# Decoding 64-bit weights: low bits taken by ScalarE, and pieces of 512 columns instead of 256 until the folding is done

## The chip, the cores and the metric

One core of one Trainium2 chip runs one launch of the kernel. The metric is device time in microseconds, from the first instruction to the end of the launch. Engines are called as in the profile: PE (TensorE; PEld is its weight load), DVE (VectorE), ACT (ScalarE), POOL (GpSimd), SP (SyncE, which here issues most of the DMAs).

## What is computed

A recurrent attention over 768 steps, for 4 batches of 8 heads with a 40x40 state each, then two dense blocks without a norm or a residual:

```python
for t in range(S):                                   # 768
    y[:, :, t] = einsum('bhd,bhde->bhe', r_t, state)
    Sa = einsum('bhde,bhe->bhd', state, a_t)
    state = state * w_t[:, :, None, :] - einsum('bhd,bhe->bhde', Sa, b_t) + einsum('bhd,bhe->bhde', v_t, k_t)
x = y as (3072 tokens, 320)
h = (x @ w1) * (x @ w2) @ w3                         # w1, w2: 320x1024, w3: 1024x1024
x = h @ w_out                                        # 1024x320
out = maximum(x @ w_in, 0) ** 2 @ w_out2             # 320x2048, 2048x320
```

The weights of the dense blocks come as 64-bit floating-point numbers (a weight is a 32-bit draw times a 64-bit scalar), everything else as 32-bit.

## The kernel before

**Stages.** The 768 steps are cut into 24 chunks of 32 (`NCH`, `C`). A chunk is a chain of small matmuls on PE with evictions between them: `do_x0` (L737), `do_sa` (L747, evicted to `SA` by ACT at L749), `do_sat` (L754, evicted at L756 and L759), `do_l` (L767, evicted to `YI` by DVE at L772), `do_z` (L780) and `do_ys` (L795, evicted by DVE: the new state at L803, the outputs at L807). `do_sa` needs a small triangular inverse, which `solve` computes on DVE for four chunks at a time: pairs of L651 and L654, step by step, and a transpose (L657) that hands the result to the chunks. `solve(0)` runs in the opening, `solve(1)` beside chunks 2 to 4. `prep` (scans on DVE at L551 and L561, products on POOL at L573 and L579) makes ready the inputs of later chunks.

**Filling.** PE's order is the order of the program (`manual_schedule`): between the chunk's matmuls `stage` pulls a given number of nanoseconds of other PE work from a queue (`Fill`). First in it is the folding, `w3 @ w_out` into one 1024x320 matrix (`fold`, `step`, the matmuls of L455): 64 steps in chunks 0 to 3. Behind it come the first dense block, in 12 tiles of 256 tokens (`a_tile`: matmuls of L366 into `ab`, `g` and `gl` on DVE at L398 and L404, `gh` on ACT, then `px` at L424). The second dense block (`ph` at L366, `po` at L992) runs after all chunks. DVE, ACT, POOL and SP are ordered by a scheduler; each then works through its list in order, and an instruction that waits holds up all behind it.

**Decoding.** `fetch` brings a piece of a weight matrix as raw 32-bit words (two for a number) and makes a 32-bit number of each pair: ACT takes the high word as a float and scales its exponent (L324), DVE shifts left by 3 and clears the sign (L326), ors in the top 3 bits of the low word (L328), and ors in the sign (L330). In the opening the three DVE steps are held back until `solve(0)` is done (`hold`, `issue_after`). The raw words lie in a ring (`raw`), except the first pieces of a kind, which are staged in memory that later holds other tiles (`staged`, tile `early`). `wo` comes in 16 pieces of 160 columns, `w3` in 32 of 256 (2 blocks of 128), `w1` and `w2` in 20 of 256, and, after the folding, `w_in` in 20 of 256 and `w_out2` in 16 of 320. The rings hold 6 raw pieces and 8 decoded ones, and 3 for `w1`/`w2` (`WB`); the first 10 pieces of `w3` are asked for before the chunks begin (`W3_FIRST`), the others one after every second folding step. `w1`, `w2` and `w_in` are then split in two parts: ACT copies one (L338, L349), POOL subtracts it from the whole (L339, L350); `w_out2` likewise (L937, L938).

Of the kernel before, what the change touches and what calls it, by code (L numbers as in the profile page):

```python
# [18 lines left out]
DM = 320  # L19
# [30 lines left out]
SPLIT_AT = (14, 22, 22, 31)  # L50
W3_FIRST = 10
FOLD_STAGED = 16
SPLIT_STAGED = 16
# [7 lines left out]
GAPE = (1300, 2400, 1700, 1600, 1600, 1300, 1000, 2400)  # L61
CUT = (7, 18)
LOOK = (1, 0, 2, 1, 5, 2)
WB = (6, 8, 3)
# [178 lines left out]
def body(tc, img, rv, rd, vn, vp, raw, w1, w2, w3t, wo, win, wo2, ident, maskt, out, dbg=None):  # L243
# [4 lines left out]
    with (  # L248
# [12 lines left out]
        with right, tc.manual_schedule(engines={mybir.EngineType.PE}):  # L261
# [8 lines left out]
            def staged(pl, tags):  # L270
# [23 lines left out]
            def fetch(pl, K, N, parts, dst=None, tag="fold"):  # L294

                place = None
                if early:
                    count[tag] += 1
                    if tag == "split" and count[tag] <= SPLIT_STAGED:
                        place = staged(ma, ("gh", "gl"))  # L300
                    elif tag == "fold" and not w12 and count[tag] <= FOLD_STAGED:
                        place = staged(wa, ("w1h", "w1l", "w2h"))
# [31 lines left out]
            def split_w(pl, src, h, l, j, k):  # L334

                t = fetch(pl, 1, 256, [(slice(0, 128), 0, wcols(src, 256 * j, 256)[128 * k:128 * k + 128])], tag="split")
                f = slice(256 * j, 256 * j + 256)
# [3 lines left out]
            def split_r(pl, two):  # L341


                t = fetch(pl, 1, 256, [(slice(64 * i, 64 * i + 64), 0, wcols(src, c, 256)[256:320])
                                       for i, (src, c, _) in enumerate(two)], tag="split")
                for i, (_, c, r) in enumerate(two):
                    p, q = slice(64 * i, 64 * i + 64), slice(64 - 64 * i, 128 - 64 * i)
                    f = slice(c, c + 256)
# [90 lines left out]
            def fold(solved):  # L439
# [5 lines left out]
                def load_w3(i):  # L445
                    f, g = i // 4, i % 4
                    w3[i] = fetch(wf, 2, 128, [(slice(0, 128), slice(0, 2), wcols(w3t, 128 * f, 128)[
                        256 * g:256 * g + 256, :].rearrange("(k p) f -> p k f", p=128))])

                def step(f, k):  # L450
# [3 lines left out]
                    i = 4 * f + k // 2  # L454
                    mm(out=ps, lhsT=w3[i][:, k % 2], rhs=wo_sb[:, k], start=(k == 0), stop=(k == 7))  # L455
# [4 lines left out]
                def split12(j):  # L460
# [17 lines left out]
                for f in range(8):  # L478
                    for k in range(8):
                        items.append((FOLD_NS, lambda f=f, k=k: step(f, k), "w"))  # L480
                        i = 4 * f + k // 2 + W3_FIRST
                        if k % 2 and i < 32:
                            items.append((0, lambda i=i: load_w3(i), "decode"))
                        if k % 2:
                            for j in range(4):
                                if SPLIT_AT[j] == 4 * f + k // 2:
                                    items.append((0, lambda j=j: split12(j), "decode"))
# [644 lines left out]
```

## Time and profile before

| | |
|---|---|
| median of 3 runs | 1086.69 us (1085.41 to 1086.9) |
| the profiled execution | 1085.28 us, its span 1083.4 us |
| PE busy | 920.8 us (85%) |
| DVE busy | 740.9 us (68%) |
| ACT busy | 420.1 us (39%) |
| POOL busy | 239.6 us (22%) |

How to read it: an engine's busy share over the whole span says little here, since the program has four stretches: the opening, chunks 0 to 3 with the folding, the other chunks filled with the first dense block, and the second dense block. The engine that sets the pace is found per stretch, from busy times by window and from the waits of PE.

### The profile page before, as it was taken

How to read it: one execution, taken by the hardware profiler on the slowest of the kernel's cores; microseconds unless marked ns; L12 is line 12 of the kernel's file. 1: busy time of each engine (PE TensorE's matmuls, PEld its weight loads, DVE VectorE, ACT ScalarE, POOL GpSimd, SP SyncE). 2: the span in 40 equal slices, each digit the busy share in tenths (PEclk: the TensorE clock that was granted, in tenths of full speed). 3: DMA queues.
4: the chain of work that ended last, by engine and by line, in shares of the span. 5: the costliest groups of instructions: out<-in, count | busy, mean ns of one | idle time of the engine just before them, and what ended most of it. 6: DMA issues, size and time to landing. Idle time of an engine off the chain costs nothing.

```text
span 1083.4 us, 29473 instructions
## 1 busy us (share of the span) xinstructions
PE 920.8 (85%) x12240; PEld 825.1 (76%) x12240; DVE 740.9 (68%) x1571; ACT 420.1 (39%) x918; POOL 239.6 (22%) x316
## 2 busy tenths in 40 slices
PE   1326768669999998988999999879999999999997
PEld 1315545558888887877898888869998989898896
DVE  6795889947985996699569544798555564434432
ACT  2313444433334434333343343565433333333332
POOL 0260234613344334433310000454000000000000
PEclk9999888879989999988999998999999999999998
DMA  8977767546657756665764453458112221000001
GB/s 204 287 201 226 192 210 194 143 143 181 149 146 178 193 154 145 165 154 141 172 155 100 113 127 73 121 163 180 30 46 64 62 48 19 7 25 1 19 7 27
DMA packets 211804, 134.46 MB, mean 124 GB/s; under 512 B 144318, under 2 KB 186687, under 8 KB 211249
## 3 DMA queue, kind: packets, MB, share of 16 engines
q1 hardware_dynamic: 204304, 110.61, 40.5%
q0 software_dynamic: 7072, 21.57, 7.1%
q8 instruction: 98, 1.61, 0.7%
q10 hardware_dynamic: 288, 0.33, 0.1%
q14 instruction: 42, 0.34, 0.1%
HBM read 99.27 MB, written 33.19 MB: 122 GB/s over the span
## 4 chain that ended last, share of the span: by engine, by line
PE 54%; DVE 22%; DMA 7%; issue 3%; ACT 2%; SPq 1%; POOL 0%; ACTq 0%; DVEq 0%
PE ph L366 17%; PE po L992 16%; PE ab L366 9%; DVE tmp L651 3%; PE px L424 3%; DVE T L654 3%; PE pat L795 3%; DMA X_d<-yst 2%; DVE RX L803 2%; DVE yst L807 2%; DMA xr<-X_d 2%; DVE wst L328 1%; DVE wst L330 1%; PE pat L780 1%; PE pat L767 1%
## 5 line engine op out<-in xcount | busy, mean ns | idle before, releaser
L992 PE MATMUL po<-wul,rh 128*128 128x320 f32 x384 | 118.4, 309 | 0.0
L992 PE MATMUL po<-wuh,rh 128*128 128x320 f32 x384 | 118.1, 308 | 0.0
L992 PE MATMUL po<-wuh,rl 128*128 128x320 f32 x384 | 117.0, 308 | 0.0
L366 PE MATMUL ab<-xh,w1h 128*128 128x256 f32 x192 | 60.5, 315 | 23.1 <-DVE g L398 22.1
L366 PE MATMUL ph<-xh,wih 128*128 128x512 f32 x192 | 76.6, 399 | 3.1 <-issue 3.1
L403 ACT CAST gh<-g 128x256 fp32r<-128x256 f32 x96 | 39.0, 406 | 99.6 <-DVE g L398 99.4
L366 PE MATMUL ph<-xh,wil 128*128 128x512 f32 x192 | 76.2, 397 | 0.0
L366 PE MATMUL ph<-xl,wih 128*128 128x512 f32 x192 | 76.1, 397 | 0.0
L992 PEld LDWEIGHTS po<-wul,rh 128*128 128x128 f32 x384 | 72.1, 188 | 4.2
L992 PEld LDWEIGHTS po<-wuh,rh 128*128 128x128 f32 x384 | 72.0, 188 | 3.8
L992 PEld LDWEIGHTS po<-wuh,rl 128*128 128x128 f32 x384 | 71.8, 188 | 0.0
L651 DVE TENSOR_TENSOR tmp<-PT,T 128x31 f32<-128x31 f32 (+20 forms) x170 | 68.6, 404 | 3.2
L579 POOL TENSOR_TENSOR im<-im,suf 104x256 f32<-104x256 f32 x80 | 66.0, 852 | 9.5 <-DVE wo_sb L328 5.0
L654 DVE TENSOR_TENSOR T<-T,tmp 128x31 f32<-128x31 f32 (+20 forms) x170 | 65.1, 383 | 2.6
L424 PE MATMUL px<-wph,gh 128*128 128x320 f32 x192 | 64.4, 336 | 2.4 <-ACT gh L403 2.4
L404 DVE TENSOR_TENSOR gl<-g,gh 128x256 fp32r<-128x256 f32 x96 | 44.3, 462 | 28.6 <-ACT gh L403 28.4
L795 PE MATMUL pat<-YI,YR 128*40 128x72 f32 (+1 forms) x1536 | 55.9, 234 | 8.3 <-DVE YI L772 4.4
L398 DVE TENSOR_TENSOR g<-a_sb,ab 128x256 f32<-128x256 f32 x96 | 39.8, 414 | 33.1 <-ACT a_sb L397 32.2
L424 PE MATMUL px<-wph,gl 128*128 128x320 f32 x192 | 60.8, 317 | 1.2 <-DVE gl L404 1.2
L795 PEld LDWEIGHTS pat<-YI,YR 128*40 128x40 f32 x1536 | 51.6, 123 | 13.4 <-issue 5.2
L397 ACT COPY a_sb<-ab 128x256 f32<-128x256 f32 x96 | 35.5, 370 | 66.1 <-PE ab L366 65.7
L366 PE MATMUL ph<-xq,wir 128*128 128x512 f32 x192 | 60.6, 397 | 0.0
(539 smaller groups left out, 2497.5 us busy)
## 6 DMA issues: line engine op xcount, KB each, us to landing
raw<-w3t SPq DMA_DIRECT2D x32, 256.0 KB
YR<-KB_d SPq DMA_DIRECT2D x48, 160.0 KB
im<-img POOLq DMA_DIRECT2D x28, 240.0 KB, 4.8
wt<-AW_d SPq DMA_DIRECT2D x24, 214.5 KB
raw<-wo SPq DMA_DIRECT2D x16, 320.0 KB
RX<-vp SPq DMA_DIRECT2D x24, 208.0 KB
vs<-rv SPq DMA_DIRECT2D x24, 208.0 KB
KB_d<-kn POOLq DMA_DIRECT2D x14, 320.0 KB, 5.5
```

Source lines behind the costliest of these rows:

```text
L366: mm(out=ps, lhsT=seq[i][0], rhs=seq[i][1], start=(i == 0), stop=(i == 7))
L397: act.copy(out=a_sb, in_=ps[:, 0])
L398: dve.tensor_tensor(out=g, in0=a_sb, in1=ps[:, 1], op=ALU.mult)
L403: act.copy(out=t["gh"][:, ff], in_=g)
L404: dve.tensor_tensor(out=t["gl"][:, ff], in0=g, in1=t["gh"][:, ff], op=ALU.subtract)
L424: mm(out=ps, lhsT=a_, rhs=b_, start=(k == 0 and i == 0), stop=(k == 7 and i == 2))
L579: eng.tensor_tensor(out=kb[:, g, :, :, j], in0=kb[:, g, :, :, j], in1=sg, op=ALU.mult)
L651: dve.tensor_tensor(out=tv, in0=Pv[:, :, s, s + 1:n].unsqueeze(3).to_broadcast(sh), in1=Tv[:, :, s, 0:s + 1].unsqueeze(2).to_broadcast(sh) ...
L654: return dve.tensor_tensor(out=o, in0=o, in1=tv, op=ALU.subtract).ins
L795: mm(out=ps[64 * y:64 * y + D, b, 72 * z:72 * z + n], lhsT=YR[:, u], rhs=YI[:, u, 0:n], start=True, stop=True, tile_position=(0, 64 * y))
L803: dve.tensor_tensor(out=o, in0=v[r, :, :, C:72], in1=decay.unsqueeze(3).to_broadcast([D, 2, HZ, D]), op=ALU.mult)
L992: mm(out=po[j][g], lhsT=a_, rhs=b_, start=(ff == 0 and i == 0), stop=(ff == 15 and i == 2))
```

## The change

It does two things. The three DVE steps of decoding become two: ACT makes the top 3 bits of the low word by arithmetic, in place on the raw words (convert to float, times 2^-29, plus a bias just above -0.5, converted back to a whole number by rounding), and one DVE instruction shifts the high part and ors these bits in; the clearing of the sign falls away, as the shift drops it. This holds for all weights. And up to the end of the folding the pieces are twice as wide: `wo` 8 of 320, `w3` 16 of 4x128, `w1` and `w2` 10 of 512. The rings are halved in pieces (3 raw, 4 decoded, 2 for `w1`/`w2`), `W3_FIRST` and the points at which `w1` and `w2` are fetched (`SPLIT_AT`) are restated in the new pieces. A staging tile now gives three places for `wo` (640 words each), so that all 8 pieces have a place; before, 12 of the 16 had one at a time.

```diff
-SPLIT_AT = (14, 22, 22, 31)
-W3_FIRST = 10
-FOLD_STAGED = 16
-SPLIT_STAGED = 16
+SPLIT_AT = (8, 13)
+W3_FIRST = 5
+FOLD_STAGED = 8
+SPLIT_STAGED = 8
+LOW = 2.0 ** -21 - 0.5
-WB = (6, 8, 3)
+WB = (3, 4, 2)
...
-                    t = pl.tile([128, 4, 512], U32, name="early", tag=tags[n[0] % len(tags)])
+                    t = pl.tile([128, 2048], U32, name="early", tag=tags[n[0] % len(tags)])
-                    slots.extend(t[:, i] for i in range(4))
+                    slots.extend(t[:, i:i + words] for i in range(0, 2049 - words, words))
...
                 act.activation(out=o, in_=hi.bitcast(F32), func=AF.Copy, scale=2.0 ** -112)
+                act.activation(out=lo, in_=lo, func=AF.Copy, scale=2.0 ** -29, bias=LOW)
                 with tc.issue_after(hold[-1]) if hold else nullcontext():
-                    dve.tensor_scalar(out=ou, in0=ou, scalar1=3, scalar2=0x7FFFFFFF, op0=ALU.logical_shift_left,
-                                      op1=ALU.bitwise_and)
-                    dve.scalar_tensor_tensor(out=ou, in0=lo, scalar=29, in1=ou, op0=ALU.logical_shift_right,
+                    dve.scalar_tensor_tensor(out=ou, in0=ou, scalar=3, in1=lo, op0=ALU.logical_shift_left,
                                              op1=ALU.bitwise_or)
...
             def split_w(pl, src, h, l, j, k):
+                n = 512 if early else 256
-                t = fetch(pl, 1, 256, [(slice(0, 128), 0, wcols(src, 256 * j, 256)[128 * k:128 * k + 128])], tag="split")
+                t = fetch(pl, 1, n, [(slice(0, 128), 0, wcols(src, n * j, n)[128 * k:128 * k + 128])], tag="split")
...
                 def load_w3(i):
-                    f, g = i // 4, i % 4
-                    w3[i] = fetch(wf, 2, 128, [(slice(0, 128), slice(0, 2), wcols(w3t, 128 * f, 128)[
+                    f, g = i // 2, i % 2
+                    w3[i] = fetch(wf, 4, 128, [(slice(0, 128), slice(0, 4), wcols(w3t, 128 * f, 128)[
...
-                for i in range(16):
-                    c = 160 * (i % 2)
-                    fetch(wf, 1, 160, [(slice(0, 128), 0, wcols(wo, c, 160)[128 * (i // 2):128 * (i // 2) + 128])],
+                for i in range(8):
+                    fetch(wf, 1, DM, [(slice(0, 128), 0, wcols(wo)[128 * i:128 * i + 128, :])], dst=wo_sb[:, i:i + 1])
```

The scheduler also sets other orders. (In the changed kernel the lines below `fetch` are shifted by 2 to 4: ACT's two decoding steps stand at L325 and L326, DVE's at L328 and L330.) Three places count. The first is ACT in the opening, around chunk 0's eviction of `do_sa` into `SA`. Before:

```order
L739 ACTIVATE X_101<-pat 128x320
L692 ACTIVATE x_759<-pat 128x128
L696 COPY tt<-pat 16x8x16 x4
L596 COPY Pn<-pat 128x2x4x32
L324 ACTIVATE wo_sb<-early 128x160 x4
L749 COPY SA<-pat 128x8x40
```

and in the changed kernel:

```order
L741 ACTIVATE X_101<-pat 128x320
L694 ACTIVATE x_683<-pat 128x128
L698 COPY tt<-pat 16x8x16 x4
L325 ACTIVATE wst<-raw 128x512
L326 ACTIVATE raw<-raw 128x512 x3
L598 COPY Pn<-pat 128x2x4x32
L326 ACTIVATE raw<-raw 128x512
L751 COPY SA<-pat 128x8x40
```

The last four pieces of `wo`, which had to wait for a staging place, no longer stand ahead of `SA`; five steps on `w3` pieces, for which a place in the raw ring must come free, now do.

The second is DVE at the end of `solve(1)`, the transpose that chunk 4 waits for. Before, from the step with 3x29 on:

```order
L654 TENSOR_TENSOR T<-T,tmp 128x3x29
L326 TENSOR_SCALAR wst<-wst 128x256
L651 TENSOR_TENSOR tmp<-PT,T 128x60
L328 SCALAR_TENSOR_TENSOR wst<-raw,wst 128x256
L654 TENSOR_TENSOR T<-T,tmp 128x2x30
L330 SCALAR_TENSOR_TENSOR wst<-raw,wst 128x256
L651 TENSOR_TENSOR tmp<-PT,T 128x31
L326 TENSOR_SCALAR wst<-wst 128x320
L654 TENSOR_TENSOR T<-T,tmp 128x31
L328 SCALAR_TENSOR_TENSOR wst<-raw,wst 128x320
L657 STREAM_TRANSPOSE tt<-T 128x8x32
```

and in the changed kernel:

```order
L809 TENSOR_TENSOR yst<-pat,wt 40x2x4x32 x2
L330 SCALAR_TENSOR_TENSOR wst<-raw,wst 128x256
L656 TENSOR_TENSOR T<-T,tmp 128x3x29
L402 TENSOR_TENSOR g<-a_sb,ab 128x256
L330 SCALAR_TENSOR_TENSOR wst<-raw,wst 128x320
L653 TENSOR_TENSOR tmp<-PT,T 128x60
L408 TENSOR_TENSOR gl<-g,gh 128x256
L656 TENSOR_TENSOR T<-T,tmp 128x2x30
L653 TENSOR_TENSOR tmp<-PT,T 128x31
L656 TENSOR_TENSOR T<-T,tmp 128x31
L402 TENSOR_TENSOR g<-a_sb,ab 128x256
L659 STREAM_TRANSPOSE tt<-T 128x8x32
```

Chunk 3's last outputs (`yst`) now stand directly ahead of the solve's last steps, not seven of its steps earlier, and the decoding steps of `w_in` and `w_out2` among them are fewer.

The third is SP's list at the same place, the first pieces of `w_in` and `w_out2` (called `wo` there). Before, behind chunk 3's output to memory:

```order
L810 DMA X_d<-yst 40x4x128
L318 DMA raw<-win 128x512 x2
L377 DMA xf<-X_d 128x2x256
L379 DMA xr<-X_d 64x256 x2
L318 DMA raw<-win 64x512 x2
L318 DMA raw<-wo 128x640 x2
```

and in the changed kernel, ahead of chunk 3's `YR` and `YI` loads and of its output:

```order
L319 DMA raw<-win 128x512 x2
L319 DMA raw<-win 64x512 x2
L602 DMA Q_d<-qt 128x256
L319 DMA raw<-wo 128x640 x2
L616 DMA KB_d<-kn 128x640
L319 DMA raw<-win 128x512
L716 DMA YR<-KB_d 64x2x320
```

These loads moved forward by a dozen DMAs.

## Rows read from the trace of the kernel before

**Rows 1.** Busy time by window: PE, PEld, DVE, ACT, POOL, clock, DMA share, GB/s.
```profile
84.00:145.00 61.00, 42.35 (x866) 31.84 (x866) 42.29 (x99) 20.94 (x56) 13.64 (x16) 0.87 0.74 207
145.00:227.00 82.00, 53.86 (x818) 40.16 (x818) 78.69 (x200) 35.52 (x90) 36.59 (x42) 0.79 0.68 189
227.00:690.00 463.00, 427.03 (x7706) 395.95 (x7707) 332.70 (x754) 180.37 (x422) 126.81 (x193) 0.95 0.57 142
690.00:726.00 36.00, 26.29 (x185) 25.04 (x184) 35.87 (x79) 21.75 (x56) 19.78 (x21) 0.95 0.56 163
726.00:760.00 34.00, 34.00 (x173) 29.99 (x174) 30.15 (x57) 20.22 (x44) 16.07 (x15) 0.95 0.80 169
```

**Rows 2.** Waits of PE, 0 to 260 us: total, times, longest.
```profile
PE pat L747 <- DVE tt L657: 14.4, 1, 14.4
PE pat L754 <- ACT SA L749: 14.2, 2, 8.2
...
PE pat L737 <- DVE RX L803: 4.4, 2, 3.2
```

**Rows 3.** DVE by form, 145 to 227 us: the decoding steps (busy, mean ns).
```profile
L330 DVE SCALAR_TENSOR_TENSOR wst<-raw,wst 128x256 uint32<-128x256 uint32 x22 | 10.8, 495 | 0.0
L328 DVE SCALAR_TENSOR_TENSOR wst<-raw,wst 128x256 uint32<-128x256 uint32 x21 | 10.6, 510 | 0.0
L326 DVE TENSOR_SCALAR wst<-wst 128x256 uint32<-128x256 uint32 x31 | 9.6, 316 | 2.0 <-ACT wst L324 1.9
L328 DVE SCALAR_TENSOR_TENSOR wst<-early,wst 128x256 uint32<-128x256 uint32 x10 | 5.0, 510 | 0.0
L330 DVE SCALAR_TENSOR_TENSOR wst<-early,wst 128x256 uint32<-128x256 uint32 x10 | 4.0, 409 | 0.0
```

**Rows 4.** Timeline of DVE: start, duration, instruction.
```profile
70.47 1.72 DVE L330 SCALAR_TENSOR_TENSOR wo_sb<-early,wo_sb 128x160 uint32<-128x160 uint32 x7
72.12 0.74 DVE L330 SCALAR_TENSOR_TENSOR wst<-raw,wst 128x256 uint32<-128x256 uint32 x2
...
186.29 0.41 DVE L328 SCALAR_TENSOR_TENSOR wst<-early,wst 128x256 uint32<-128x256 uint32 x1
186.63 0.28 DVE L326 TENSOR_SCALAR wst<-wst 128x256 uint32<-128x256 uint32 x1
186.83 0.41 DVE L654 TENSOR_TENSOR T<-T,tmp 128x255 f32<-128x255 f32 x1
```

**Rows 5.** Timeline of DVE at the end of `solve(1)`: waits in brackets.
```profile
223.90 0.29 DVE L326 TENSOR_SCALAR wst<-wst 128x256 uint32<-128x256 uint32 x1 [1.92 <-ACT wst L324]
```

**Rows 6.** POOL by form, 145 to 227 us: the subtractions that split `w2`.
```profile
L339 POOL TENSOR_TENSOR w2l<-wst,w2h 128x256 fp32r<-128x256 f32 x8 | 7.9, 996 | 12.9 <-PE pat L688 9.6 <-ACT w2h L338 3.2
```

**Rows 7.** Timelines of ACT and DVE in chunk 0.
```profile
77.73 0.35 ACT L324 ACTIVATE wo_sb<-early 128x160 f32<-128x160 f32 x1 [5.89 <-DMA early<-wo]
...
80.33 0.41 ACT L749 COPY SA<-pat 128x320 f32<-128x320 f32 x1
...
89.60 1.39 DVE L772 TENSOR_TENSOR YI<-pat,msk 64x512 f32<-64x512 f32 x2
```

**Rows 8.** Waits of PE, 690 to 727 us.
```profile
PE ab L366 <- DVE g L398: 5.2, 2, 3.6
PE ph L366 <- issue: 3.1, 1, 3.1
```

**Rows 9.** DVE by form, 690 to 726 us: the step that goes.
```profile
L326 DVE TENSOR_SCALAR wst<-wst 128x256 uint32<-128x256 uint32 x11 | 5.5, 502 | 0.0
...
L326 DVE TENSOR_SCALAR wst<-wst 128x320 uint32<-128x320 uint32 x8 | 3.7, 460 | 0.0
```

**Rows 10.** ACT by form, whole span: the decoding step on ACT (mean ns).
```profile
L324 ACT ACTIVATE wst<-raw 128x256 f32<-128x256 f32 x56 | 24.4, 439 | 33.9 <-DMA raw<-win 11.2 <-PE pw L455 10.0 <-DMA raw<-w3t 8.0
...
L324 ACT ACTIVATE wo_sb<-early 128x160 f32<-128x160 f32 x16 | 5.6, 347 | 21.6 <-DMA early<-wo 20.9
```

**Rows 11.** Timeline of DVE at the change to the second block.
```profile
725.32 0.50 DVE L429 STREAM_TRANSPOSE x<-px 128x320 f32<-128x320 f32 x1
```

More of the change, by code (lines that the diff above doesn't have):

```diff
@@ L299, in fetch @@
                     if tag == "split" and count[tag] <= SPLIT_STAGED:
-                        place = staged(ma, ("gh", "gl"))
+                        place = staged(ma, ("gh", "gl"), 1024)
                     elif tag == "fold" and not w12 and count[tag] <= FOLD_STAGED:
-                        place = staged(wa, ("w1h", "w1l", "w2h"))
+                        place = staged(wa, ("w1h", "w1l", "w2h"), 640)
                 tag = "split" if early and tag == "split" else "wst"
@@ L334, in split_w @@
             def split_w(pl, src, h, l, j, k):
-                t = fetch(pl, 1, 256, [(slice(0, 128), 0, wcols(src, 256 * j, 256)[128 * k:128 * k + 128])], tag="split")
-                f = slice(256 * j, 256 * j + 256)
+                n = 512 if early else 256
+                t = fetch(pl, 1, n, [(slice(0, 128), 0, wcols(src, n * j, n)[128 * k:128 * k + 128])], tag="split")
+                f = slice(n * j, n * j + n)
                 act.copy(out=h[:, k, f], in_=t[:, 0])
@@ L341, in split_r @@
             def split_r(pl, two):
-                t = fetch(pl, 1, 256, [(slice(64 * i, 64 * i + 64), 0, wcols(src, c, 256)[256:320])
+                n = 512 if early else 256
+                t = fetch(pl, 1, n, [(slice(64 * i, 64 * i + 64), 0, wcols(src, c, n)[256:320])
                                        for i, (src, c, _) in enumerate(two)], tag="split")
@@ L347, in split_r @@
                     p, q = slice(64 * i, 64 * i + 64), slice(64 - 64 * i, 128 - 64 * i)
-                    f = slice(c, c + 256)
+                    f = slice(c, c + n)
                     act.copy(out=r[p, f], in_=t[p, 0])
@@ L453, in step @@
                     ps = w3["ps"]
-                    i = 4 * f + k // 2
-                    mm(out=ps, lhsT=w3[i][:, k % 2], rhs=wo_sb[:, k], start=(k == 0), stop=(k == 7))
+                    i = 2 * f + k // 4
+                    mm(out=ps, lhsT=w3[i][:, k % 4], rhs=wo_sb[:, k], start=(k == 0), stop=(k == 7))
                     if k == 7:
@@ L466, in split12 @@
                             split_w(wf, src, *t[0:2], j, k)
-                    split_r(wf, [(src, 256 * j, t[2]) for src, t in zip((w1, w2), w12)])
+                    split_r(wf, [(src, 512 * j, t[2]) for src, t in zip((w1, w2), w12)])
                 hold.append(solved)
-                for i in range(16):
-                    c = 160 * (i % 2)
-                    fetch(wf, 1, 160, [(slice(0, 128), 0, wcols(wo, c, 160)[128 * (i // 2):128 * (i // 2) + 128])],
-                          dst=wo_sb[:, i // 2:i // 2 + 1, c:c + 160])
+                for i in range(8):
+                    fetch(wf, 1, DM, [(slice(0, 128), 0, wcols(wo)[128 * i:128 * i + 128, :])], dst=wo_sb[:, i:i + 1])
                 for i in range(W3_FIRST):
@@ L480, in fold @@
                         items.append((FOLD_NS, lambda f=f, k=k: step(f, k), "w"))
[L481 to L486, printed above, removed]
+                        i = 2 * f + k // 4
+                        if k % 4 == 3:
+                            if i + W3_FIRST < 16:
+                                items.append((0, lambda i=i + W3_FIRST: load_w3(i), "decode"))
+                            for j in range(2):
+                                if SPLIT_AT[j] == i:
                                     items.append((0, lambda j=j: split12(j), "decode"))
```

4 lines of the change are left out of this document (2 added, 2 removed).

## The prediction

> **What bounds the kernel now.** The page's totals say PE, 85% busy, but totals mix stretches, so I first read busy time by window [rows 1]. From 726 us to the end PE works without a gap; from 227 to 690 us it works 427 of 463 us. What the change does to DVE can't be worth much there. From 145 to 227 us it is different: DVE works 78.7 of 82 us and PE only 53.9. That is chunks 2 and 3 with the rest of the folding, while `solve(1)` runs in between. From 690 to 726 us, where the last tile of the first block meets the decoding of `w_in` and `w_out2`, DVE works 35.9 of 36 us and PE 26.3. So the second view is what PE waits for [rows 2]: once 14.4 us at `do_sa` of chunk 4 for the last transpose of `solve(1)`, 4.4 us for the new state of a chunk, both by DVE. And DVE in these stretches is for a large part decoding: 31 + 31 + 32 steps between 145 and 227 us with 40.0 us busy [rows 3]. The order's fences show why that delays others: decoding steps stand between the steps of the solve, and DVE works through its list in order.
>
> **What a step costs.** Durations overlap a little, so I take start to start in an undisturbed piece of the timeline [rows 4]. The two-operand steps: seven of 160 columns in 72.12 - 70.47 = 1.65 us, 0.236 each; one of 256 in 186.63 - 186.29 = 0.34. The 96 columns between them cost 0.104, 1.08 ns a column, and 0.063 us is fixed. One of 512 is then 0.063 + 0.554 = 0.62 us (an estimate, no such step is in the trace). The step with one operand, L326, takes 186.83 - 186.63 = 0.20 us.
>
> **The change, part by part.**
>
> *145 to 227 us.* Removed are 31 L326. At 0.20 each that is 6.2 us; at their busy time, which holds what neighbours cost them, 9.6 [rows 3]. The 63 two-operand steps become half as many of double width: some 31 times the fixed 0.063, 2.0 us. Together 8.2 to 11.6 us. DVE is full and in order here, PE waits for its results, so I let it through to the end of the stretch: **-9**. What would take its place is PE, but that has 28 us of slack in this window [rows 1].
>
> *The end of `solve(1)`.* DVE there waited 1.92 us for a piece of `w_in` whose load SP had only just issued [rows 5], with the last solve steps behind it. In the changed order these loads stand ahead of chunk 3's own, and fewer decoding steps stand among the solve's last. **-2**, bounds 0 and -2; chunk 3's outputs that now stand in front cost nothing anew, since the same work was done in the same stretch.
>
> *84 to 145 us.* DVE works 42.3 of 61 us [rows 1]; some 16 L326 go here too, but the rest of the time it waits for loads and for PE, and so a shorter step mostly ends in a longer wait. **-1**, bounds 0 and -5 (16 times the 0.28 of [rows 4] and a few joins).
>
> *Chunk 0.* Before, ACT waited 5.89 us for one of the last four `wo` pieces, whose staging place came free late, and `SA` stood behind it: it began at 80.33 [rows 7], and PE waited 8.2 us [rows 2]. That wait goes, since all eight pieces now have a place. But ahead of `SA` now stand steps on five raw places that have to come free. I worked it through: the ring's first three pieces are decoded last of the held batch (8 `wo` and 3 `w3` pieces, two DVE steps each, with transposes and a scan some 14 us behind the solve), then three loads of 512 KB follow, and the last of the five needs one more turn of decode and load. That gives about 83 us, later by 3. PE's next stop in the chunk, `YI`, began at 89.60 [rows 7], behind scans, so there is room for about that. **0**, bounds -4 and +4.
>
> *690 to 726 us.* 19 L326 go: 9.2 us busy [rows 9], at least 19 times 0.20, 3.8. PE is idle 36 - 26.3 = 9.7 us here, of which 5.2 are waits for `g` on DVE and 3.1 end at the first `ph` [rows 8], right behind a transpose that stood in DVE's list behind decoding [rows 11]. **-5**, bounds 0 and -8. The widths don't change here.
>
> *ACT.* It gains a step for each piece. The trace has no ACT step that reads and writes whole numbers; the nearest is its own decoding step, 439 ns at 256 columns and 347 at 160 [rows 10], 0.96 ns a column, hence 0.69 us at 512 (an estimate). I take that, with twice as much as the upper bound and nothing below. From 145 to 227 us ACT comes from 35.5 us to about 44 of 82 (16 low steps of 0.69, and 31 of 0.44 become 16 of 0.69). From 690 to 726 us it comes from 21.8 to 30.6 of 36 (11 of 0.44, 8 of 0.50): nearly full, but no longer the same engine as the solve or `g`. From 726 to 760 us 12 to 14 more steps make 26 of 34, beside a PE without a gap, whose evictions ACT makes: **0**, bounds 0 and +3.
>
> *Clock.* PE's granted clock is 0.79 between 145 and 227 us, after waits like the 14.4 us one, and 0.95 behind [rows 1]. Shorter waits may give some of that back: counted as 0, with -3 in the range.
>
> *POOL.* Its subtractions get twice as wide and half as many. A step of 256 takes 996 ns on average [rows 6], and DVE steps beside POOL are longer: the 63 two-operand steps have 30.4 us in all [rows 3], against 63 times the 0.409 of the undisturbed group, 25.8; L326 lost another 1 us. So 5.6 us of DVE's time went on sharing. I count it unchanged, since the same bytes are subtracted. The Trainium skill, "SBUF — State Buffer", section "SBUF: two separate sides", speaks against that: DVE with two SBUF inputs and GpSimd take a shared port pair as an exclusive lock, "starts first gets the pair for the whole instruction; the other fully blocks". By that rule a DVE step that meets a subtraction would wait twice as long as before, half as often met by count but for the same share of time. It has a case of its own below.
>
> **The sum.** -9 - 2 - 1 - 5 = -17 us. Against the profiled execution (span 1083.4, time 1085.28) that is 1068.3; the median of the runs is 1.4 higher than that execution, so I forecast **1070 us**. Everything behind 227 us moves as a whole, since chunks 4 to 23 are near PE's limit and their order on PE is the same.
>
> **The rivals.**
> *Hidden anyway.* The pieces themselves set the pace: DMA is busy 0.68 to 0.74 of 84 to 227 us, the ring has three pieces instead of six, and what DVE saves it spends waiting for ACT, which waits for a load (as in [rows 5]). Against it: DVE was idle only 3 of 82 us. Then only the change of blocks at 690 us remains, and a little: -5, 1081.7. 15%.
> *POOL holds DVE longer.* If half as many subtractions of twice the length hold a DVE step twice as long, the 5.6 us of sharing double: 1070 + 6 = 1076. For it: L328 takes 510 ns on average against 409. Against: the waits also shrink with the L326 that no longer takes part. 13%. (It is the case in which the page's rule decides.)
> *Slower: ACT's list blocks the chunks.* Low-bit steps wait for loads of 512 KB that have to find a place in a ring of three, and `X0`, `SA` and `vs` of chunks 0 to 3 stand behind them. Such a block cost 8.2 and 14.2 - 8.2 = 6.0 us before [rows 2]. Four new ones of 6 us would be 24 us, 7 more than the gain: 1093.7. It takes three to cancel the gain; the point from which it decides is a load that lands after `do_sa` of its chunk is done on PE. For it: the order in chunk 0. Against: from chunk 1 on the list has mostly the first step of a piece, not the load, ahead of `SA`. 12%.
> *The step on ACT is not what it seems.* If whole numbers in and out cost ACT twice the time, 690 to 726 us would be full of ACT instead of DVE, and the -5 would go, with some of the -9: about 1080. 3%.
>
> **How the numbers follow.** The forecast has 57%. Its own range is 1060 to 1079: all bounds in its favour would give 1054 and all against it 1086, but they won't fall together. Widened to the rivals, 1058 to 1086 leaves out the slower case and a tail below. What a measurement here can tell from no change is about 0.2%, 2.2 us: faster by more has 80% (the forecast but for its upper end, the sharing case, most of the hidden one), within it 7%, slower 13%.
>
> **What would show it.** Right: DVE's busy time falls by some 40 us in all; the 14.4 us wait for `tt` is under 6; chunk 4's `do_sa` begins near 216 instead of 227 us; the first `ph` comes about 17 us earlier than 725.9, and the length from there to the end is the same. Wrong: `SA` of chunk 0 far behind 83 us or new waits on ACT for `raw` loads in chunks 1 to 3 (the slower case); DVE idle between 145 and 227 us (hidden); two-operand steps with a mean far above 0.75 us (sharing).

## The result, and the profile after

| | before | after |
|---|---|---|
| median, measured together | 1086.42 us (1085.41 to 1086.9, 4 runs) | 1072.54 us (1067.19 to 1078.62, 4 runs) |
| ratio | | 0.9887, interval 0.9847 to 0.9927 |
| the profiled execution, its span | 1085.28, 1083.4 us | 1078.62, 1076.7 us |
| PE, DVE, ACT, POOL busy | 920.8, 740.9, 420.1, 239.6 us | 917.4, 714.0, 442.1, 233.3 us |

The change is faster by 13.9 us where 16.7 were forecast. Two things make that less clean than it looks. The profiled execution after is the slowest of its four, only 6.7 us under the profiled one before. And the kernel after scatters over 11 us where the one before scattered over 1.5. In later comparisons the changed kernel came out at 0.9931 and 0.9932, 6 to 7 us. The experiments below had to say which part of the gain is the change's.

First the stretches: busy time by window of the profile after (the columns of [rows 1]: PE, PEld, DVE, ACT, POOL, clock, DMA share, GB/s).

```profile
84.00:145.00 61.00, 42.68 (x940) 32.36 (x939) 39.57 (x74) 27.73 (x62) 11.95 (x14) 0.88 0.75 207
145.00:227.00 82.00, 60.62 (x969) 47.90 (x968) 70.67 (x136) 42.52 (x91) 31.59 (x33) 0.86 0.69 187
227.00:690.00 463.00, 422.72 (x7594) 392.05 (x7593) 336.81 (x760) 180.74 (x424) 130.99 (x197) 0.96 0.58 142
690.00:726.00 36.00, 29.86 (x176) 27.34 (x175) 33.95 (x61) 29.55 (x83) 21.03 (x22) 0.91 0.62 189
```

From 145 to 227 us DVE fell by 8.0 us and PE did 6.8 us more. ACT went from 35.5 to 42.5 us; about 44 was forecast. Next the waits of PE up to 260 us (total, times, longest).

```profile
PE pat L756 <- ACT SA L751: 18.0, 3, 8.7
...
PE pat L797 <- ACT kn L615: 6.3, 1, 6.3
...
PE pat L739 <- DVE RX L805: 3.4, 3, 2.0
...
PE pat L769 <- ACT vs L758: 3.0, 3, 1.9
...
PE pat L749 <- DVE tt L659: 1.6, 1, 1.6
```

The 14.4 us wait for the last transpose of `solve(1)` [rows 2] is down to 1.6. In its place waits for ACT have grown: `SA` 18.0 where it was 14.2, 6.3 for `kn` in chunk 2, and `vs`, 1.9 of it in chunk 4. The longest one for `SA`, in chunk 2, isn't behind a low-bit step: two casts of the first block's input stand ahead of it on ACT and wait 3.85 and 1.59 us for their loads, as they did before (4.16 and 2.26).

The decoding steps of DVE by form, 145 to 227 us, and lines of the timelines of DVE and POOL (start, duration), answer to [rows 3]:

```profile
L330 DVE SCALAR_TENSOR_TENSOR wst<-raw,wst 128x512 uint32<-128x512 uint32 x9 | 8.7, 969 | 0.1
L328 DVE SCALAR_TENSOR_TENSOR wst<-wst,raw 128x512 uint32<-128x512 uint32 x9 | 6.8, 752 | 0.0
...
L328 DVE SCALAR_TENSOR_TENSOR wst<-wst,early 128x512 uint32<-128x512 uint32 x4 | 3.8, 955 | 0.1
...
L330 DVE SCALAR_TENSOR_TENSOR wst<-early,wst 128x512 uint32<-128x512 uint32 x4 | 3.2, 802 | 0.0
```

```profile
170.59 1.45 POOL L341 TENSOR_TENSOR w1l<-wst,w1h 128x512 fp32r<-128x512 f32 x1
170.83 1.75 DVE L328 SCALAR_TENSOR_TENSOR wst<-wst,early 128x512 uint32<-128x512 uint32 x1
...
179.37 0.69 DVE L328 SCALAR_TENSOR_TENSOR wst<-wst,early 128x512 uint32<-128x512 uint32 x1
...
190.05 2.39 DVE L330 SCALAR_TENSOR_TENSOR wst<-raw,wst 128x512 uint32<-128x512 uint32 x1
```

A mean hides two kinds here. Of the 26 steps 20 take 0.64 to 0.69 us, and six take 1.07 to 2.39. Those six hold 8.9 us, 4.8 more than six at 0.68. Each of the six ends 0.54 to 0.56 us after the end of a POOL instruction that runs beside it, as in the first two lines: POOL until 172.04, DVE until 172.58. Four of these instructions are subtractions, two are products for `im`, whose size did not change.

ACT's new step (by form, 145 to 227 us) costs what the older step suggested; 0.69 was estimated at 512 columns:

```profile
L326 ACT ACTIVATE raw<-raw 128x512 uint32<-128x512 uint32 x8 | 5.4, 678 | 10.1 <-DMA raw<-w3t 4.0 <-DMA raw<-w 3.0 <-DVE wst L330 2.3
L326 ACT ACTIVATE raw<-raw 128x256 uint32<-128x256 uint32 x6 | 2.7, 450 | 4.9 <-DMA raw<-win 4.9
```

Last the stretch from the outputs of chunk 23 to the first `ph`, which is the handover: busy time by window (671.6 to 718.8 us, columns as above), then PE's waits in it.

```profile
671.60:718.80 47.20, 38.45 (x309) 36.34 (x308) 41.59 (x77) 35.40 (x95) 25.85 (x28) 0.93 0.58 159
```

```profile
PE ab L370 <- DVE g L402: 4.2, 3, 2.2
PE px L428 <- ACT gh L407: 1.0, 2, 0.8
PE px L428 <- DVE gl L408: 0.7, 2, 0.5
```

It takes 47.2 us; before it took 46.5 (from 679.4 to 725.9). Here the prediction had its -5.

**The gain stage by stage.** Starts on PE from the timelines, against the profiled execution before. Two more profiles of the changed kernel (`after_again`, `after_pair`) stand beside the first, because one profile of a kernel that scatters by 11 us can mislead. The parts are differences of the places in the next table, which are rounded to 0.1 us; the five of a column sum to the difference of its span.

| us against before | forecast | after | after_again | after_pair |
|---|---|---|---|---|
| up to `do_sa` of chunk 4 | -12 | -12.1 | -10.5 | -10.9 |
| from there to `do_ys` of chunk 4 (16.1 before) | 0 | +2.1 | +1.3 | +6.1 |
| to `do_ys` of chunk 23 (436.1 before) | 0 | +2.2 | -2.2 | +2.3 |
| to the first `ph` (46.5 before) | -5 | +0.7 | +0.5 | -0.1 |
| to the end (357.5 before) | 0 | +0.4 | +0.5 | +0.2 |
| span | -17 | -6.7 | -10.4 | -2.4 |

The first row is one wait. `do_x0` of chunk 4 begins at 206.4 us after the change and at 206.65 before, so chunks 1 to 3 did not end earlier; what is shorter is PE's wait for the transpose behind it.

### The profile page after: what moved, and what is told of

Same layout as the page of the kernel before. It is cut to its first block, busy times and chain, and to the rows that moved or that the text cites. A ratio compares the mean times of both kernels' runs of the same rounds, so it can differ in the third digit from the quotient of the medians.

```text
span 1076.7 us, 29204 instructions
## 1 busy us (share of the span) xinstructions
PE 917.4 (85%) x12240; PEld 823.3 (76%) x12240; DVE 714.0 (66%) x1399; ACT 442.1 (41%) x942; POOL 233.3 (22%) x304
## 4 chain that ended last, share of the span: by engine, by line
PE 52%; DVE 23%; DMA 12%; issue 4%; ACT 4%; SPq 2%; POOL 2%; ACTq 0%; DVEq 0%; POOLq 0%
PE ph L370 15%; PE po L994 15%; PE ab L370 9%; PE px L428 4%; DVE tmp L653 4%; DVE T L656 4%; PE pat L797 2%; DVE wst L328 2%; DVE yst L809 2%; DVE RX L805 2%; DMA im<-img 2%; DMA raw<-w3t 2%; PE pat L769 2%; DMA AW_d<-wi 2%; PE pat L782 1%
## 5 line engine op out<-in xcount | busy, mean ns | idle before, releaser
L653 DVE TENSOR_TENSOR tmp<-PT,T 128x31 f32<-128x31 f32 (+20 forms) x170 | 64.9, 382 | 3.5
L797 PEld LDWEIGHTS pat<-YI,YR 128*40 128x40 f32 x1536 | 53.1, 125 | 16.1 <-ACT kn L615 7.3
L428 PE MATMUL px<-wpl,gh 128*128 128x320 f32 x192 | 60.9, 317 | 0.0
```

The costliest lines, as they stand in the source:

```text
L428: mm(out=ps, lhsT=a_, rhs=b_, start=(k == 0 and i == 0), stop=(k == 7 and i == 2))
L653: dve.tensor_tensor(out=tv, in0=Pv[:, :, s, s + 1:n].unsqueeze(3).to_broadcast(sh), in1=Tv[:, :, s, 0:s + 1].unsqueeze(2).to_broadcast(sh) ...
L797: mm(out=ps[64 * y:64 * y + D, b, 72 * z:72 * z + n], lhsT=YR[:, u], rhs=YI[:, u, 0:n], start=True, stop=True, tile_position=(0, 64 * y))
```

## Experiments

The first two rows are the comparison above. All others were timed beside the kernel before again, in three groups in which it had medians of 1083.75 (after_again to late_old), 1085.31 (late_low to first3_late_old) and 1083.57 us (the rest). The times, and the places in each profile, in us:

| run | median (runs) | ratio, interval | `do_sa` 4 | `do_ys` 4 | `do_ys` 23 | first `ph` | span |
|---|---|---|---|---|---|---|---|
| before | 1086.42 (4) | | 227.2 | 243.3 | 679.4 | 725.9 | 1083.4 |
| after | 1072.54 (4) | 0.9887, 0.9847 to 0.9927 | 215.1 | 233.3 | 671.6 | 718.8 | 1076.7 |
| after_again | 1077.87 (11) | 0.9931, 0.9903 to 0.9959 | 216.7 | 234.1 | 668.0 | 715.0 | 1073.0 |
| low_only | 1075.94 (10) | 0.9920, 0.9888 to 0.9953 | 215.9 | 233.4 | 670.9 | 716.8 | 1074.8 |
| sizes_only | 1081.33 (12) | 0.9969, 0.9945 to 0.9993 | 225.0 | 241.0 | 680.7 | 728.8 | 1086.4 |
| late_old | 1073.02 (6) | 0.9889, 0.9849 to 0.9929 | 218.2 | 234.1 | 666.4 | 713.0 | 1069.7 |
| late_low | 1086.34 (12) | 1.0011, 0.9985 to 1.0036 | 226.8 | 243.7 | 683.1 | 729.9 | 1086.7 |
| pool_halves | 1079.43 (12) | 0.9937, 0.9917 to 0.9956 | 216.4 | 236.9 | 674.4 | 720.8 | 1079.3 |
| high_twice | 1072.95 (6) | 0.9900, 0.9867 to 0.9932 | 214.1 | 231.4 | 665.9 | 713.1 | 1070.7 |
| first3_late_old | 1074.37 (6) | 0.9903, 0.9879 to 0.9927 | 218.3 | 234.9 | 668.8 | 716.7 | 1073.4 |
| after_pair | 1076.93 (12) | 0.9932, 0.9910 to 0.9954 | 216.3 | 238.5 | 676.9 | 723.3 | 1081.0 |
| late_old_pair | 1077.71 (9) | 0.9924, 0.9888 to 0.9961 | 216.8 | 233.5 | 670.8 | 718.8 | 1076.4 |
| ring44 | 1073.78 (6) | 0.9903, 0.9866 to 0.9941 | 218.9 | 237.3 | 667.6 | 714.8 | 1071.5 |
| no_late_sub | 1071.43 (1) | | 217.5 | 234.8 | 668.6 | 713.6 | 1069.6 |

My theory going in: DVE's relief in chunks 2 and 3 carries the gain. The rivals: the wider pieces carry it; the handover gives it; ACT's list takes part of it back.

**The changed kernel again (`after_again`).** No edit.

> The changed kernel itself, once more, because its first four executions lie 11 us apart (1067.2 to 1078.6) and those of the kernel before only 1.5. Theory (the gain is DVE's in chunks 2 and 3 and stays; what varies is the granted clock and the blocks at the handover): a median of 1069 to 1074 us; chunk 4's do_sa again within 2 us of 215; the first ph anywhere between 712 and 719, and 357 to 358 us from there to the end. Rival (the first profile was typical and the gain is 7 us): a median of 1077 to 1080. Second rival (the loads of 512 KB land at other times each run, and the chunks move with them): chunk 4's do_sa moves by 5 us or more between the two profiles.

The median was 1077.9, between the theory and the rival; the eleven runs go from 1069.5 to 1081.2. `do_sa` of chunk 4 at 216.7 is within 2 us of the first profile, so the early gain stands and the loads' timing is not what varies. The kernel before was less steady here too (1075.5 to 1090.8 in 26 runs).

**The low bits alone (`low_only`).** The kernel before with

```diff
+                act.activation(out=lo, in_=lo, func=AF.Copy, scale=2.0 ** -29, bias=LOW)
-                    dve.tensor_scalar(out=ou, in0=ou, scalar1=3, scalar2=0x7FFFFFFF, ...)
-                    dve.scalar_tensor_tensor(out=ou, in0=lo, scalar=29, in1=ou, ...)
+                    dve.scalar_tensor_tensor(out=ou, in0=ou, scalar=3, in1=lo, ...)
```

> Part one alone: ScalarE makes the low bits and DVE needs two steps a piece, with the pieces, the ring and the staging of the kernel before. Theory (the relief of DVE by L326 carries the gain): 6 to 10 us from chunks 2 and 3 and up to 5 from 690 to 726 us, 1072 to 1080 us in all; wait for tt before chunk 4 under 9 us. Rival (the wider pieces carry it): 1083 to 1087. Rival (ACT's list blocks the chunks): with six raw places and small loads no new block of 6 us; if it is slower than 1086 then the ACT step itself costs the chain.

**The sizes alone (`sizes_only`).** The changed kernel with the three DVE steps of before.

> Part two alone: pieces of 512 (wo 320) columns, the ring of three and the new staging, with DVE's three steps a piece and no low bits on ACT. Theory: only the fixed part of half the steps goes (some 31 + 16 times 0.06 in chunks 2 and 3, and 15 to 20 in chunk 0), 2 to 5 us: 1081 to 1085 us; the wait for tt stays over 8 us. Rival (the wider pieces carry the gain): 1070 to 1077. Rival (fewer and longer loads in a ring of three block ACT, chunks late): over 1088.

The low bits alone bring 7.8 us on the medians and `do_sa` of chunk 4 from 227.2 to 215.9. The sizes alone bring 2.4 and 2.2. The wait for `tt` is gone in the first (no such row) and stays in the second, in its waits of PE up to 260 us:

```profile
PE pat L750 <- DVE tt L660: 12.9, 1, 12.9
```

So the step that left DVE carries the gain, as the sum had it. The wider pieces bring some 2 us alone and nothing on top of it: the whole change measured 1.9 us above low_only in the same group, within the intervals. The scheduler set a new order in each of these runs, so the step and the order that follows from it are priced together.

**The late pieces as before (`late_old`, `late_old_pair`).** The changed kernel, with the new decoding only `if early:`; what comes after the folding keeps three DVE steps. **The late pieces alone (`late_low`)** is the complement: the kernel before, with the new decoding only `if not early:`.

> The changed kernel, but w_in and w_out2 after the folding (all that is decoded in pieces of 256 from 600 us on) get the three DVE steps of before and no low bits on ACT. It prices the step of the prediction on the handover. Theory as forecast (the handover is worth 5 us): 4 to 6 us slower than the changed kernel on the same chip. Rival (the handover is worth nothing, as the first profile has it: 46.5 us from the last chunk's outputs to the first ph before, 47.2 after): within 2 us of it.

> The complement of the run late_old: the kernel before, with ScalarE's low bits and DVE's two steps only for w_in and w_out2, which are decoded in pieces of 256 and 320 after the folding. It prices this part alone. The forecast's own term was 5 us faster (1079 where the kernel before has 1084). Theory formed from late_old (with it the change is 4.9 us faster in the median): in the handover DVE saves nothing, because three more pieces find room ahead of the first ph, and behind it rl waits for rh behind low-bit steps on ACT, some 2 us: between no change and 4 us slower than before; ys of chunk 23 to the first ph 46 to 48 us; PE idle 1.5 us or more in the 38 us behind the first ph.

> late_old again, beside the changed kernel: three DVE steps for w_in and w_out2 as before. Theory (the late low bits are worth nothing or cost 1 to 4 us, and the earlier 4.9 us between the medians was in part the clock's): 0 to 4 us faster than after_pair; again 46 to 47 us from chunk 23's outputs to the first ph. Rival (the late low bits are a gain, as the prediction had it): 3 us or more slower than after_pair.

> The changed kernel, for a comparison on one chip with late_old_pair and ring44. From the runs so far (ratios to before of 0.9887 and 0.9931): 0.989 to 0.994. If the scatter is the granted clock's, its runs lie over 6 us or more, and in the profile the chunks from 5 on lose or gain time only where the granted clock of the stretch differs.

The late part is no gain in the totals: alone it measures 1.0 us slower, 1.6 us faster to 3.9 slower by its interval. Leaving it out gave 4.9 us less than the changed kernel in the first group, which neither expectation had, and 0.8 more in the third, where 0 to 4 less were expected; so whether it costs something is not settled by the totals. The traces show what happens. In late_old, 666.4 to 713.04 us, the handover is that of the kernel before almost to the digit, 46.6 us with PE busy 36.53 (36.60 before). In late_old_pair it took 48.0, not the 46 to 47 expected, at a lower granted clock:

```profile
666.40:713.04 46.64, 36.53 (x309) 34.66 (x309) 42.64 (x91) 27.68 (x72) 23.52 (x26) 0.96 0.53 146
```

```profile
670.80:718.80 48.00, 37.65 (x310) 35.92 (x309) 43.04 (x91) 27.52 (x72) 23.68 (x26) 0.93 0.52 142
```

With the low bits on ACT the length looks the same (46.4 to 47.2 us in the three profiles of the changed kernel), but all three ran at 0.93 there, so they have to be set beside the profiles with three steps at 0.93: late_old_pair, sizes_only and first3_late_old, 47.9 to 48.1. At 0.96 low_only, which has the low bits too, stands beside the kernel before and late_old, 45.9 against 46.5 and 46.6:

```profile
670.90:716.80 45.90, 36.96 (x310) 34.87 (x309) 41.61 (x77) 35.33 (x95) 25.76 (x28) 0.96 0.59 163
```

So at equal clock the late low bits shorten the handover by some 1 us (0.6 to 1.7), and PE's idle time in it falls from 9.9 to 10.4 us to 8.4 to 8.9. They cost as much or more at two further places. One is chunk 4. Its ACT timeline in after_pair (waits in brackets) and PE's wait behind it:

```profile
225.04 0.43 ACT L326 ACTIVATE raw<-raw 128x256 uint32<-128x256 uint32 x1 [4.00 <-DMA raw<-win]
225.37 0.57 ACT L758 COPY vs<-pat 104x512 f32<-104x512 f32 x1
```

```profile
225.99 1.97 PE L769 MATMUL pat<-RT,vs 104*64 104x64 f32 x32 [3.90 <-ACT vs L758]
```

The low bits of the first pieces of `w_in` wait for their load, and `vs` stands behind them in ACT's list: 1.9, 1.4 and 3.9 us of PE in the three profiles of the changed kernel, 0.8 in late_low, and no such wait in chunk 4 of the two profiles of late_old. The other is the start of the second block, where `rh` stands between decoding steps (waits of PE after the change, 718 to 760 us); before and in late_old there is no such row, and late_low has 0.8 us of it, where 1.5 or more were expected.

```profile
PE po L994 <- DVE rl L981: 1.7, 2, 1.5
```

**POOL's subtractions in halves (`pool_halves`).** In `split_w`, and in the same way in `split_r`:

```diff
-                pool.tensor_tensor(out=l[:, k, f], in0=t[:, 0], in1=h[:, k, f], op=ALU.subtract)
+                for c in range(0, n, 256):
+                    q = slice(n * j + c, n * j + c + 256)
+                    pool.tensor_tensor(out=l[:, k, q], in0=t[:, 0, c:c + 256], in1=h[:, k, q], op=ALU.subtract)
```

> The changed kernel with POOL's subtractions of 512 columns cut in two of 256, the same bytes. It tests whether the length of a POOL step is what a DVE step waits for. Theory of the Trainium skill's rule (a DVE step waits for the whole POOL instruction): the 26 two-operand steps of 512 in chunks 2 and 3, 0.87 us on average now against 0.62 alone, come down towards 0.75, 2 to 4 us in all, and chunk 4's do_sa begins 2 to 4 us earlier, at 211 to 213. Rival (the sharing goes by the bytes and not by the instruction): the mean stays within 0.05 us of 0.87, and chunk 4 within 1.5 us of 215 to 217.

DVE by form, 145 to 227 us:

```profile
L330 DVE SCALAR_TENSOR_TENSOR wst<-raw,wst 128x512 uint32<-128x512 uint32 x9 | 7.9, 876 | 0.1
L328 DVE SCALAR_TENSOR_TENSOR wst<-wst,raw 128x512 uint32<-128x512 uint32 x9 | 6.8, 754 | 1.3 <-ACT wst L325 1.3
L328 DVE SCALAR_TENSOR_TENSOR wst<-wst,early 128x512 uint32<-128x512 uint32 x4 | 3.2, 808 | 1.1 <-ACT wst L325 1.0
L330 DVE SCALAR_TENSOR_TENSOR wst<-early,wst 128x512 uint32<-128x512 uint32 x4 | 3.2, 802 | 0.0
```

The 26 steps now take 21.1 us, 0.81 each, against 22.5 and 0.87: a drop of 0.06, between the theory's 0.12 and the rival's 0.05. Seven of them are long now where six were, each by less. Chunk 4 does not begin earlier (216.4) and the total is that of the changed kernel. The length of a POOL step is worth at most 1.4 us of DVE here, and nothing at the end.

**ACT's first step twice (`high_twice`).** The line of L325 written a second time, `if early:`.

> The changed kernel with ACT's first decoding step done twice (same data, same place) until the folding is done: some 40 more ACT steps of 0.67 or 0.49 us, about 24 us of ACT's busy time, 17 of it between 84 and 227 us. It prices a busier ACT by itself. Theory (ACT's own length is not on the path; its waits for loads are): chunk 4's do_sa at most 4 us later than 215 to 217, total within 4 us of the changed kernel. Rival (ACT became the engine that sets chunks 0 to 3): chunk 4 and the total 10 us or more later.

Chunk 4's `do_sa` came at 214.1, no later, although ACT was busy 50.0 us between 145 and 227 us instead of 42.5:

```profile
145.00:227.00 82.00, 61.08 (x1050) 48.07 (x1050) 74.40 (x142) 49.99 (x105) 31.48 (x35) 0.94 0.62 171
```

So 7.5 us more of ACT's work need not cost anything. It isn't the same order with a busier ACT, though: the scheduler put the first piece of `w_in` behind `vs` of chunk 4 on ACT (219.6 us, 198.8 after), PE waited 7.6 us for `SA` up to 260 us where it waited 18.0, and the last transpose of `solve(1)` began 8.4 us earlier than after:

```profile
205.97 0.64 DVE L661 STREAM_TRANSPOSE tt<-T 128x256 f32<-128x256 f32 x1
```

That `do_sa` of chunk 4 still came only 1.0 us earlier than after shows that little more is to be had from DVE here: the transpose was there 7.5 us before it. Its ratio of 0.9900 lies below the changed kernel's 0.9931 and 0.9932, but the intervals overlap, and with another order I take no gain from it.

**Fewer pieces asked for ahead (`first3_late_old`).** late_old with `W3_FIRST = 3`.

> The run late_old with three instead of five pieces of w3 in the held batch, so that fewer low-bit steps with their waits for loads stand ahead of SA of chunk 0 on ACT. Theory (these blocks cost chunk 0, 9 us of PE's waiting for SA): SA of chunk 0 begins before 79 us instead of 83, and do_sa of chunk 1 1 to 4 us earlier than the 102.8 to 104.3 now; of this up to 3 us may reach the end, 0 to 3 us faster than late_old. Rival (scans and loads hold YI anyway): chunk 1 within 1 us, no difference in the total. Against both: the folding starts later and chunk 4 waits for it, slower.

A miss: `SA` of chunk 0 began at 84.19 (84.72 in late_old), and chunk 1 at the same 104.3. Fewer pieces ahead do not free ACT there. The rival's "no difference in the total" holds (0.9903 against 0.9889 and 0.9924).

**The handover (`ring44`, `no_late_sub`).** ring44 is the changed kernel with `BB = (4, 4)` for `(5, 4)`. no_late_sub leaves out POOL's subtractions for `wil` and `wul` and lets PE read `wih` and `wuh` in their place.

> The changed kernel with four raw places instead of five for w_in and w_out2. By the order 19 decoded pieces instead of 21 then stand on DVE between the outputs of chunk 23 and the last transpose ahead of the first ph (18 in the kernel before). Theory (what DVE saved in the handover went into three more pieces placed ahead of that transpose): 47 us from the outputs to ph become 43 to 45, and 0 to 3 us come off the total if the pieces behind ph do not stop PE. Rival (POOL's subtractions set the pace of the handover, whatever stands in the list): still 46 us or more.

> The changed kernel without POOL's subtractions for the low parts of w_in (its first 256 rows) and w_out2; the products that would read them read the high parts, so PE's work is the same and the output lacks these low parts. 20 of the 28 POOL steps of the handover go. Theory (DVE's decoding steps there are mostly waits beside POOL: two-operand steps of 256 take 0.59 to 0.62 us on average against 0.34 alone): they come down to 0.35 to 0.48, and the stretch from the outputs of chunk 23 to the first ph falls from 47 us to 40 to 43, although 23 pieces now stand ahead. Rival (PE and the chain of transposes set it): 46 us or more.

Their handovers by window (667.6 to 714.8 and 668.6 to 713.6 us), ring44's first:

```profile
667.60:714.80 47.20, 38.94 (x310) 37.21 (x309) 38.14 (x73) 33.68 (x90) 23.89 (x27) 0.89 0.57 158
```

```profile
668.60:713.60 45.00, 38.04 (x309) 35.04 (x309) 35.39 (x81) 36.13 (x101) 6.91 (x8) 0.96 0.64 180
```

In ring44 DVE did fall, 41.6 to 38.1 us, but its transposes now wait for PE (waits of DVE in that window), and the stretch is as long as in the changed kernel, though at a clock of 0.89 instead of 0.93; PE's idle time in it is 8.3 us against 8.8:

```profile
DVE x L433 <- PE px L428: 2.8, 2, 2.0
```

DVE by form in no_late_sub, the same window:

```profile
L328 DVE SCALAR_TENSOR_TENSOR wst<-wst,raw 128x256 uint32<-128x256 uint32 x13 | 6.2, 480 | 2.6 <-ACT wst L325 1.6 <-ACT raw L326 1.0
...
L330 DVE SCALAR_TENSOR_TENSOR wst<-raw,wst 128x256 uint32<-128x256 uint32 x13 | 5.4, 419 | 0.1
```

The means of two-operand steps fell to 0.48 and 0.42 us at 256 columns (0.62 and 0.59 after), DVE's busy time by 6.2 us, and the stretch by 2.2 only, where the theory wanted 4 to 7; at its clock of 0.96 low_only has 45.9 us, 0.9 more. This is one execution. PE's idle time in it is 7.0 us (45.00 - 38.04), against 8.8 after (47.20 - 38.45) and 9.9 before (46.5 - 36.6). So POOL's subtractions and the third step together hold some 3 of PE's 9.9 idle us; about 7 stay, with DVE still busy for 35.4 of the 45 us. What is left is waits for `g`, `gh` and `gl` of the last half tiles, which go PE, ACT, DVE, ACT, DVE, PE one after the other; that this chain alone makes the 7 us is argued, not tried.

## Why the prediction was right, and where it wasn't

**145 to 227 us (-9) and the end of `solve(1)` (-2): right in sum and place, not in the second mechanism.** `do_sa` of chunk 4 came 10.5 to 12.1 us earlier in three profiles; -12 was forecast with the -1 of the stretch ahead. low_only shows that the removed step carries it. DVE's busy time there fell by 8.0; 8.2 to 11.6 was worked out. The rival "hidden anyway" falls with it: of 14.4 us of waiting 1.6 are left. From 145 us to the start of the last transpose DVE was busy 78.1 us before and 64.3 after, 11.8 of the difference in decoding steps. The -2 was to come from a shorter wait for loads. That wait of 1.92 us is gone, but DVE's idle time ahead of the transpose went up, from 3.3 to 5.1 us. In its place the scheduler moved two scans, which make ready later chunks and which the order fences don't show, from ahead of the transpose to behind it (timeline of DVE, before and after), worth some 2.5 us:

```profile
212.55 1.25 DVE L551 TENSOR_TENSOR_SCAN suf<-iw,mark 104x529 f32<-104x529 f32 x1
216.66 1.25 DVE L561 TENSOR_TENSOR_SCAN wi<-iw,inv 104x528 f32<-104x528 f32 x1
...
226.44 0.60 DVE L657 STREAM_TRANSPOSE tt<-T 128x256 f32<-128x256 f32 x1
```

```profile
214.35 0.60 DVE L659 STREAM_TRANSPOSE tt<-T 128x256 f32<-128x256 f32 x1
214.81 1.20 DVE L553 TENSOR_TENSOR_SCAN suf<-iw,mark 104x529 f32<-104x529 f32 x1
...
217.57 1.26 DVE L563 TENSOR_TENSOR_SCAN wi<-iw,inv 104x528 f32<-104x528 f32 x1
```

**Chunk 0 (0): right.** `SA` began at 83.17 where 83 was forecast, and the second stop had the room: `YI` at 88.15, 1.4 us earlier than in [rows 7]. ACT after, in chunk 0:

```profile
82.60 0.67 ACT L326 ACTIVATE raw<-raw 128x512 uint32<-128x512 uint32 x1 [2.12 <-DMA raw<-w3t]
83.17 0.40 ACT L751 COPY SA<-pat 128x320 f32<-128x320 f32 x1
```

**POOL (0): right, though not by the bytes.** Taking 0.68 us as a 512-column step alone, sharing cost the 26 steps 4.8 us; the 63 before had 4.6 by the same count, and L326 another 1. The Trainium skill, "SBUF — State Buffer", section "SBUF: two separate sides", has the shared port pair as a lock held for the whole instruction. The trace agrees: every one of the six long steps ends 0.54 to 0.56 us after a POOL instruction's end, about the 0.55 that 512 columns take at 1.08 ns each. What didn't come is the doubling that the rival drew from it. A hold was longer (0.80 us a long step, about 0.5 before), but it met fewer steps: six of 26 are long, ten of 63 before.

**ACT's step: right.** 0.68 us measured, 0.69 estimated; high_twice shows that a busier ACT can be borne.

**Clock (0, with -3 in the range):** the granted clock from 145 to 227 us was 0.86 where it was 0.79; what that gave back no run separates.

**690 to 726 us (-5): wrong; about -1 in its place.** The prediction read 9.7 us of PE's idle time there as waiting for a DVE that is busy with decoding. Three profiles give +0.7, +0.5 and -0.1 against the profiled execution before; at equal clock it is some 1 us less. PE ran at 0.93 instead of 0.96 there and was busy 1.8 us longer with the same 309 matmuls; late_old_pair, sizes_only and first3_late_old, with DVE's three steps, had 0.93 as well. Two things replaced the rest of the gain. More pieces moved in: the scheduler put 21 pieces instead of 18 on DVE's list between the outputs of chunk 23 and the last transpose ahead of `ph`, so DVE's busy time fell only from 42.7 to 41.6 us. And, as ring44 and no_late_sub show, a DVE that is freer by 3 or 6 us shortens the stretch by nothing or by 1 to 2, because most of PE's idle time isn't DVE's load. The term should have been bounded by what PE waits for decoding steps, not by its idle time.

**"Everything behind 227 us moves as a whole": wrong by 1 to 6 us in chunk 4.** The rival in which ACT's in-order list blocks the chunks had its mechanism right and the place too early. Such blocks stand in chunks 0 and 2 too (`SA` and `kn` behind decoding steps), but inside the measured -12. What cost time behind it is `vs` of chunk 4, behind low-bit steps on `w_in`: 1.9, 1.4 and 3.9 us of the 2.1, 1.3 and 6.1 lost there. The rest of the 6.1 goes with the clock: 0.77 in that chunk of after_pair, 0.88 before. Three chunks had to be blocked by 6 us to cancel the gain, and that didn't happen. From chunk 4's outputs to chunk 23's PE was busy 400.5 us before and 400.7, 394.6 and 402.8 in the three profiles. The clock (0.95 before, then 0.95, 0.97 and 0.95) goes with the -2.2 of the second; the +2.2 of the first is idle time of PE that no run here explains.

**726 us and on (0, bounds 0 and +3): inside the bounds**, with 1.7 us of waits for `rl`; the length from the first `ph` to the end grew by 0.2 to 0.5.

**The total.** The steps as measured sum to between -2.4 and -10.4 us in three profiles, and the medians give -13.9, -5.9 and -6.6. The first comparison is nearest to the forecast, but a part of that nearness isn't explained by the steps: with about 1 us in the handover and 1 to 6 us given back in chunk 4, the traces bear out the 6 to 7 us of the two larger comparisons rather than 14. That the number came out within 3 us is in part luck; what made the first four executions fast is open. The prediction held 0.2%, 2.2 us, to be enough to tell a change from none; the kernel before alone then spread over 15 us in 26 runs, and the medians of the change over 8.

**The signs named in advance.** Three of the signs of being right hold: the wait for `tt` (1.6 us), `do_sa` of chunk 4 (215.1) and the length behind the first `ph`. Two don't: the first `ph` came 7.1 us earlier in the first profile and not 17, and DVE's busy time fell by 26.9 us and not by some 40. Two signs of the rivals showed without deciding: low-bit steps on ACT waited 10.0 us for loads of `w3` between 84 and 227 us, and the two-operand steps took 0.87 us on average, over 0.75.

## What to carry to other kernels

Taking one step out of a saturated in-order engine paid here where another engine demonstrably waits for that list (14.4 us for one transpose), and little elsewhere (1 us of the 5 forecast in the handover); idle time of PE beside a busy DVE is not yet time that DVE owes. When work goes to another in-order engine, look less at its busy time (50 of 82 us went without a loss in high_twice) than at what it will wait for, and at who stands behind it: a cheap step that needs a load cost up to 3.9 us of PE in chunk 4. Compare stages of two profiles at the same granted clock: 0.93 instead of 0.96 made a gain of 1 us look like none. And when a scheduler fills the list, count after the change how many steps now stand ahead of the one that matters.

## What the runs showed of the hardware

The granted clock goes with much of the scatter: within the groups the slower runs mostly have the lower mean clock. Chunk 20's stretch on PE, in the kernel before (601.0 to 621.6 us) and in sizes_only (596.9 to 622.4), columns as above:

```profile
601.00:621.60 20.60, 19.01 (x333) 17.77 (x332) 10.11 (x23) 7.03 (x16) 0.00 (x0) 1.00 0.51 121
```

```profile
596.90:622.40 25.50, 23.29 (x333) 21.71 (x332) 10.10 (x23) 7.03 (x16) 0.00 (x0) 0.80 0.41 98
```

The same 333 matmuls, the same steps on DVE and ACT, no POOL: 19.0 us of PE at 1.00 (2.4 GHz throughout), 23.3 at 0.80 (a part of it at 1.2 GHz), and 4.9 us of span. What PE did ahead of the drop I did not isolate. Such drops fall into different chunks in each execution; from chunk 4's outputs to chunk 23's the profiles of the table take 430 to 440 us with nearly the same work. That makes a difference of 3 us between two profiles unreadable except stage by stage.

A DVE step with a single operand waited for POOL as well. L326, 0.28 us long undisturbed [rows 4], took 0.50 on average in the handover before [rows 9]. Eight of its twenty steps there are long, 0.60 us or more, and each of these ends 0.15 to 0.19 us after the end of a POOL subtraction that was running when it began, as here (POOL until 713.06, DVE until 713.22):

```profile
711.01 2.05 POOL L938 TENSOR_TENSOR wul<-wst,wuh 128x320 fp32r<-128x320 f32 x2 [0.98 <-ACT wuh L937]
```

```profile
712.25 0.97 DVE L326 TENSOR_SCALAR wst<-wst 128x256 uint32<-128x256 uint32 x1
```

The same section of the Trainium skill names steps with two SBUF inputs, or in a 2-port mode, as those that share. L326 reads one operand; that its 256 columns take 0.20 us from start to start, where a two-operand step takes 0.34 [rows 4], would fit the faster mode, but no run here shows which mode it ran in.
